# Retention outputs emitted in two steps with the state part last, and one weight block cast in four slices

## The chip, the cores and the metric

The kernel runs on one core of one Trainium2 chip. The metric is the device time of one execution on that core, in microseconds. "Span" is the time from the first to the last instruction in the profile; it is about 1.7 us shorter than the device time.

## The reference, cut to what matters

```python
# q, k, v: (8 batches, 8 heads, 576, 64), w_in: (512, 2048), w_out: (2048, 512)
scores = scale * np.matmul(q, k.transpose(0, 1, 3, 2))
ret = scores * Dmat[None]              # causal decay, gamma[h] ** (i - j) for i >= j
attn = np.matmul(ret, v)               # retention
x = attn.transpose(0, 2, 1, 3).reshape(8 * 576, 512)
r = np.maximum(x @ w_in, 0.0)
out = (r * r) @ w_out                  # feed-forward with squared ReLU
```

Retention over 576 positions is computed in chunks of 128: a masked product inside the chunk, plus a product of q with a state R that carries what came before the chunk. 4608 rows of x then go through the two dense layers, which are most of the work.

## The kernel before: the parts that matter

The program is a list of tasks for a scheduler that decides, before the program is built, in which order each engine gets them. A task has an engine, a key (the smallest key of the ready tasks goes first), an estimated duration, the tasks that it depends on, and buffers that it acquires. On the chip each engine then works in exactly that order, and waits on semaphores where the estimates were too short. So an edit of one task's key or duration can move instructions of other tasks.

Eight weight blocks of 1 MB are loaded as fp32 and cast to fp16, half by GpSimd (POOL in the profile), half by ScalarE (ACT):

```python
def add_weight(i):                      # blocks 0-3: w_in, 4-7: w_out
    ...
    halves = []
    for j, eng in enumerate(("POOL", "ACT")):
        rows, sl = (slice(0, 4), slice(256 * j, 256 * j + 256)) if i == 0 else (slice(2 * j, 2 * j + 2), slice(0, 512))

        def fc(eng=eng, rows=rows, sl=sl):
            s = tile_of["w", i]
            (nc.gpsimd.tensor_copy if eng == "POOL" else nc.scalar.copy)(out=dst[:, rows, sl], in_=s[:, rows, sl])
        key = -50 + i if i or j == 0 else -17.5
        halves.append(add(eng, key, 1.05 if eng == "POOL" else 1.0, fc, deps=[t]))
    sched.free("wst", halves)           # the staging buffer goes back
    wcast[i] = halves
```

For the first four groups of rows ("pairs") the retention outputs psO are one task of TensorE. The calls of inter need the state R; the loop of 32 small matmuls in the middle needs only the masked scores rx and the values vx:

```python
def fo():
    tile_of["psO", g] = ps_ret.tile([P, 2, 512], FP32, name="psO", tag="prO")
    inter(1)                            # with the state R
    nc.tensor.drain()
    for m in range(NP):                 # rx times vx: no state
        ...
    inter(0)                            # with the state before
t = add("PE", base + 24, 1.3, fo, deps=masked + [T["R", u]] + ([T["R", u - 1]] if carry else []), acq=("prO",))
```

The second dense layer of a group runs as two chains of 16 matmuls po, one for each half s of its rows. Matmul fi reads weight block 4 + fi // 4:

```python
for s, u in enumerate(us):
    ...
    for fi in range(NF):
        ...
        f2.append(add("PE", base2 + NF * s + fi, 0.216, f, deps=[sq[fi // nf]] + wcast[4 + fi // 4] + f2[-1:],
                      acq=("ff",) if fi == 0 else ()))
```

Last, wT is a set of weight differences that later groups use (they compute the layer with fewer products, Strassen's way). VectorE (DVE) works them out once all four w_out blocks are cast, and some of them sooner, between other work.

## Time and profile before

Before: 292.55 us median of 3 runs (292.39 to 292.78). The profile's own lines stand in the prediction. What they say about the start of the kernel fits into one table: when each weight block is ready in fp16 (end of POOL's half of the cast, start plus duration; ScalarE's half ends no later), and when TensorE starts the first matmul that reads it.

| block | POOL's cast ends, us | first matmul that reads it, us | slack |
|---|---|---|---|
| w_in 1 | 20.63 + 1.04 = 21.67 | 23.09 | 1.42 |
| w_in 2 | 23.55 + 1.04 = 24.59 | about 24.83 (16 matmuls of 0.109 after 23.09) | 0.24 |
| w_in 3 | 26.25 + 1.04 = 27.29 | 27.35 | a wait |
| w_out 0 | 28.95 + 1.04 = 29.99 | 30.41 | 0.42 |
| w_out 1 | 31.65 + 1.15 = 32.80 | 33.02 | 0.22 |
| w_out 2 | 34.32 + 1.04 = 35.36 | 35.63 | 0.27 |
| w_out 3 | 37.10 + 1.29 = 38.39 | 38.45 | a wait |

It is to be read as a row of gates. TensorE passes each gate no sooner than the block has landed and been cast.

### The profile page before, as it was taken

What the parts mean: (1) busy time and instruction counts of PE and PEld (TensorE: products, weight loads), DVE (VectorE), ACT (ScalarE), POOL (GpSimd) and SP (SyncE); (2) the same over time, 40 slices, a digit from 0 to 9 for tenths busy, and PEclk for the clock granted to TensorE, in tenths of its full rate; (3) what the DMA queues carried; (4) which work ended last, traced back from release to release, by engine and by line L of the source; (5) the groups of instructions that cost most, each with busy time, mean ns of one, the idle gap of its engine ahead of it and who ended that gap; (6) DMA issues with size and microseconds to landing.
All of it is one profiled execution on the core that took longest, in us unless ns stands there. A gap on an engine that the chain in (4) does not pass through costs nothing.

```text
span 290.9 us, 10062 instructions
## 1 busy us (share of the span) xinstructions
PE 283.0 (97%) x4328; PEld 234.0 (80%) x4328; DVE 195.0 (67%) x430; ACT 187.5 (64%) x354; POOL 88.9 (31%) x123
## 2 busy tenths in 40 slices
PE   7989999999999999999999999999999999999994
PEld 2557765688888888888888888888888888888883
DVE  3796589748485848656868857667786865565632
ACT  6456966296757575867666666766767676747830
POOL 5343454524434234251616041615151400000000
PEclk9999999999999999999999999999999999999999
DMA  7999999999999899997998599979896820201004
GB/s 201 327 368 387 370 276 250 239 220 186 233 214 214 185 148 247 221 186 189 196 208 180 126 192 211 202 183 180 211 188 171 159 74 2 74 3 72 2 2 144
DMA packets 139421, 54.13 MB, mean 186 GB/s; under 512 B 118129, under 2 KB 130929, under 8 KB 139377
## 3 DMA queue, kind: packets, MB, share of 16 engines
q1 hardware_dynamic: 139072, 53.23, 81.9%
q8 instruction: 34, 0.56, 0.9%
q10 hardware_dynamic: 304, 0.26, 0.3%
q14 instruction: 11, 0.08, 0.1%
HBM read 36.70 MB, written 9.44 MB: 159 GB/s over the span
## 4 chain that ended last, share of the span: by engine, by line
PE 89%; DMA 6%; SPq 1%; issue 1%; POOL 1%; DVE 0%; DVEq 0%; POOLq 0%
PE ph L827 42%; PE po L916 34%; PE po L865 5%; PE psO L343 4%; DMA wi<-in_moe_w_in_dram 3%; DMA pair<-in_q_dram 3%; PE psc L343 2%; PE psS L343 2%; SPq L298 1%; POOL w_in L322 1%; PE psT L418 1%; DVE o L939 0%; POOL qx L403 0%; DVE p L968 0%; DVEq L939 0%
## 5 line engine op out<-in xcount | busy, mean ns | idle before, releaser
L827 PE MATMUL ph<-xT,w_in 128*128 128x256 f16 x1152 | 139.4, 273 | 0.2 <-POOL w_in L322 0.2
L827 PEld LDWEIGHTS <-w_in 128*128 128x128 f16 x1152 | 111.1, 98 | 14.8 <-POOL w_in L322 0.4
L835 ACT ACTIVATE rl<-ph 128x512 f16<-128x512 f32 x144 | 84.3, 589 | 46.9 <-PE ph L827 45.0
L845 ACT ACTIVATE gT<-rl 128x512 f16<-128x512 f16 x104 | 65.6, 631 | 3.0
L916 PEld LDWEIGHTS <-gS 128*128 128x128 f16 x512 | 49.4, 98 | 6.1 <-DVE gS L893 0.2
L916 PE MATMUL po<-wT,gS 128*128 128x256 f16 x384 | 52.4, 273 | 0.0
L893 DVE TENSOR_TENSOR gS<-gT,gS 128x512 f16<-128x512 f16 x64 | 35.1, 554 | 11.6 <-ACT gT L845 11.0
L916 PEld LDWEIGHTS <-gT 128*128 128x128 f16 x384 | 37.2, 98 | 4.4
L893 DVE TENSOR_TENSOR gS<-gT 128x512 f16<-128x512 f16 x64 | 30.7, 481 | 12.9 <-ACT gT L845 12.9
L916 PE MATMUL po<-w_out,gT 128*128 128x256 f16 x256 | 34.5, 273 | 0.0
L355 POOL CAST kq<-q 128x512 f16<-128x512 f32 x28 | 18.8, 673 | 45.7 <-DMA q<-in_q_dram 45.5
L367 POOL TENSOR_TENSOR v<-v,vdec_full 128x512 f16<-128x512 f32 x24 | 26.2, 1093 | 19.6 <-DMA v<-in_v_dram 14.4
L355 POOL CAST kq<-k 128x512 f16<-128x512 f32 x28 | 18.6, 666 | 44.4 <-DMA k<-in_k_dram 41.7
L847 DVE TENSOR_TENSOR gT<-rl 128x512 f16<-128x512 f16 x40 | 18.9, 473 | 14.7 <-ACT rl L835 14.2
L929 ACT COPY u<-po 128x256 f32<-128x256 f32 x32 | 11.8, 369 | 20.4 <-PE po L916 20.4
L939 DVE TENSOR_TENSOR o<-po,u 128x256 f32<-128x256 f32 x31 | 13.0, 421 | 16.2 <-PE po L916 8.3
L704 DVE TENSOR_TENSOR xT<-psO,gam_full 128x512 f16<-128x512 f32 x28 | 18.9, 686 | 7.5 <-PE psO L343 7.4
L643 DVE TENSOR_TENSOR rT<-psc,mask 128x512 f16<-128x512 f32 x28 | 18.3, 683 | 5.5 <-PE psc L343 5.2
L916 PE MATMUL po<-w_out,gS 128*128 128x256 f16 x128 | 17.0, 273 | 0.0
L916 PE MATMUL po<-wT,gT 128*128 128x256 f16 x128 | 16.8, 273 | 0.0
L939 DVE TENSOR_TENSOR o<-po,p 128x256 f32<-128x256 f32 x17 | 7.2, 424 | 13.7 <-ACT u L929 7.1
L865 PE MATMUL po<-w_out,gT 128*128 128x512 f16 x64 | 15.8, 380 | 0.0
(81 smaller groups left out, 244.1 us busy)
## 6 DMA issues: line engine op xcount, KB each, us to landing
out_dram<-o SPq DMA_DIRECT2D x31, 256.0 KB, 3.0
k<-in_k_dram SPq DMA_DIRECT2D x24, 256.0 KB, 4.5
q<-in_q_dram SPq DMA_DIRECT2D x24, 256.0 KB, 4.8
v<-in_v_dram SPq DMA_DIRECT2D x24, 256.0 KB, 5.3
wi<-in_moe_w_in_dram SPq DMA_DIRECT2D x4, 1024.0 KB, 10.1
wo<-in_moe_w_out_dram SPq DMA_DIRECT2D x4, 1024.0 KB, 9.7
pair<-in_k_dram SPq DMA_DIRECT2D x4, 512.0 KB, 7.0
pair<-in_q_dram SPq DMA_DIRECT2D x4, 512.0 KB, 7.0
```

The lines of the kernel that those rows point to most:

```text
L343: nc.tensor.matmul(out_, lhsT=lhsT, rhs=rhs, start=start, stop=True, skip_group_check=True, tile_position=(64 * row, 64 * col))
L355: op(out=out_.rearrange("p (n b a d) -> p n b a d", n=2, b=2, a=2), in_=in_.rearrange("p (n a b) d -> p n b a d", n=2, a=2))
L367: nc.gpsimd.tensor_tensor(out=t, in0=tile_of["v32", u], in1=vdec[kind].rearrange("p (h o) -> p h o", o=1).to_broadcast([P, H, D]), op=ALU. ...
L704: nc.vector.tensor_tensor(out=tile_of["x", g][:, :, s * P:(s + 1) * P].rearrange("p n (c i) -> p c n i", c=2), in0=tile_of["psO", g][:, :, ...
L827: nc.tensor.matmul(tile_of["ph", g, fb][:, j, :], lhsT=w_in16[:, m, fi * P:(fi + 1) * P], rhs=tile_of["x", g][:, m, :], start=(m == 0), st ...
L835: nc.scalar.activation(out=t, in_=tile_of["ph", g, fb], func=ACTF.Relu)
L845: nc.scalar.activation(out=t, in_=rl, func=ACTF.Square)
L847: nc.vector.tensor_tensor(out=t, in0=rl, in1=rl, op=ALU.mult)
L865: nc.tensor.matmul(tile_of["po", u], lhsT=tile_of["g", g][:, fi, s * P:(s + 1) * P], rhs=w_out16[:, fi, :], start=(fi == 0), stop=(fi == N ...
L893: nc.vector.tensor_tensor(out=Sx(k, h), in0=in0(h), in1=in1(h), op=op)
L916: nc.tensor.matmul(tile_of["pb", g, bank], lhsT=left(i), rhs=right[:, i, :], start=(start and i == 0), stop=(i == HF - 1), skip_group_chec ...
L939: nc.vector.tensor_tensor(out=o_tile(u)[:, half * HM:(half + 1) * HM], in0=bank(x), in1=tile_of[name, g], op=ALU.add)
```

## The change

Its intent: the 32 products that need no state are to run while VectorE still works on R, so that less TensorE work is left behind R, and the dense matmuls start sooner. So that the second weight block is no obstacle then, its cast is cut into four slices, and the first matmuls wait only for the slice that they read. The key of the first pair's R is raised too. Left out are the keys of the casts (ScalarE's raised by 0.1, and so on slice by slice) and the estimated durations of the slices, divided by 1.85. The core of the diff:

```diff
+    NARROW = (1,)
...
-        for j, eng in enumerate(("POOL", "ACT")):
-            rows, sl = (slice(0, 4), slice(256 * j, 256 * j + 256)) if i == 0 else (slice(2 * j, 2 * j + 2), slice(0, 512))
+        narrow = i in NARROW
+        for j, eng in enumerate(("POOL", "ACT", "POOL", "ACT") if narrow else ("POOL", "ACT")):
+            rows, sl = ((slice(0, 4), slice(128 * j, 128 * j + 128)) if narrow else
+                        (slice(0, 4), slice(256 * j, 256 * j + 256)) if i == 0 else (slice(2 * j, 2 * j + 2), slice(0, 512)))
...
-            chain.append(add("DVE", base + 5.6 + s, 0.5, fr2, deps=[t] + chain[-1:], acq=("R",)))
+            chain.append(add("DVE", base + (6.5 if u == 0 else 5.6) + s, 0.5, fr2, deps=[t] + chain[-1:], acq=("R",)))
...
-        def fo():
+        def fo1():
+
             tile_of["psO", g] = ps_ret.tile([P, 2, 512], FP32, name="psO", tag="prO")
-            inter(1)
-            nc.tensor.drain()
             for m in range(NP):
...
+        def fo2():
             inter(0)
-        t = add("PE", base + 24, 1.3, fo, deps=masked + [T["R", u]] + ([T["R", u - 1]] if carry else []), acq=("prO",))
+            nc.tensor.drain()
+            inter(1)
+        t = add("PE", base + 23.9, 0.6, fo1, deps=masked + T["kvx", u], acq=("prO",))
+        t = add("PE", base + 24, 0.75, fo2, deps=[t, T["R", u]] + ([T["R", u - 1]] if carry else []))
...
-        return w[:1] if fi < 2 else w
+        return w[fi % 4:fi % 4 + 1] if fi // 4 in NARROW else w[:1] if fi < 2 else w
```

More of the change, by code (lines that the diff above doesn't have):

```diff
@@ L322, in fc @@
                 (nc.gpsimd.tensor_copy if eng == "POOL" else nc.scalar.copy)(out=dst[:, rows, sl], in_=s[:, rows, sl])
-            key = -50 + i if i or j == 0 else -17.5
-            halves.append(add(eng, key, 1.05 if eng == "POOL" else 1.0, fc, deps=[t]))
+            key = -50 + i + 0.1 * j if i or j == 0 else -17.5
+            halves.append(add(eng, key, (1.05 if eng == "POOL" else 1.0) / (1.85 if narrow else 1), fc, deps=[t]))
         sched.free("wst", halves)
```

## The prediction

> **What bounds the kernel now.** I read the page first, then who waited for whom on TensorE, then the timelines of TensorE and of the engines that feed it from 14 to 40 us, because an order listing of the two programs shows no instruction moved after about 57 us.
>
> ```profile
> span 290.9 us, 10062 instructions
> PE 283.0 (97%) x4328; PEld 234.0 (80%) x4328; DVE 195.0 (67%) x430; ACT 187.5 (64%) x354; POOL 88.9 (31%) x123
> PE   7989999999999999999999999999999999999994
> ...
> GB/s 201 327 368 387 370 276 250 239 220 186 233 214 214 185 148 247 221 186 189 196 208 180 126 192 211 202 183 180 211 188 171 159 74 2 74 3 72 2 2 144
> ```
>
> TensorE is busy for 97% of the span, so no other engine's total matters; what can be won is the part in which it is not yet fed. One slice is 7.3 us: only the first four hold less than full work, and they also hold 40 warming matmuls that give nothing. In the second to fifth slice the transfers run at 327 to 387 GB/s, by far their highest: inputs and eight weight blocks of 1 MB come in as fast as this program ever moves data.
>
> ```profile
> PE psO L343 <- DVE R L489: 0.9, 1, 0.9
> PE ph L827 <- POOL w_in L322: 0.2, 1, 0.2
> ```
>
> These two are the waits of TensorE that the change can touch: one for the state R ahead of the outputs of the second pair, one for a weight cast. Now the same in order of time:
>
> ```profile
> 20.02 1.04 PE L247 MATMUL warm<-junk 128*128 128x512 f16 x4
> 22.00 0.31 PE L343 MATMUL psO<-kqT,R 64*64 64x128 f16 x8 [0.94 <-DVE R L489]
> 22.41 0.64 PE L343 MATMUL psO<-rx,vx 64*64 64x128 f16 x32
> 22.87 0.29 PE L343 MATMUL psO<-kqT,R 64*64 64x128 f16 x8
> 23.09 4.10 PE L827 MATMUL ph<-xT,w_in 128*128 128x256 f16 x36
> 27.35 3.23 PE L827 MATMUL ph<-xT,w_in 128*128 128x256 f16 x28 [0.15 <-POOL w_in L322]
> ...
> 36.50 1.91 PE L827 MATMUL ph<-xT,w_in 128*128 128x256 f16 x16
> 38.45 3.18 PE L865 MATMUL po<-w_out,gT 128*128 128x512 f16 x14
> ```
>
> From 23.09 on TensorE has real work with one gap of 0.15 us. The columns are start, duration, engine, line, what it writes from what, count, and in brackets the idle time before. The outputs psO hold TensorE from 22.00 to 23.09, and the 32 products in the middle of them do not need R. What feeds it:
>
> ```profile
> 20.93 1.02 DVE L489 TENSOR_TENSOR R<-stmp,dec 128x256 f16<-128x256 f32 x1
> 20.63 1.04 POOL L322 CAST w_in<-wi 128x1024 f16<-128x1024 f32 x1 [1.56 <-DMA wi<-in_moe_w_in_dram]
> 23.55 1.04 POOL L322 CAST w_in<-wi 128x1024 f16<-128x1024 f32 x1 [1.88 <-DMA wi<-in_moe_w_in_dram]
> 28.95 1.04 POOL L322 CAST w_out<-wo 128x1024 f16<-128x1024 f32 x1 [1.66 <-DMA wo<-in_moe_w_out_dram]
> 36.80 0.69 DVE L778 TENSOR_TENSOR wT<-w_out 128x1024 f16<-128x1024 f16 x1
> 37.10 1.29 POOL L322 CAST w_out<-wo 128x1024 f16<-128x1024 f32 x1 [1.74 <-DMA wo<-in_moe_w_out_dram]
> ```
>
> Every weight cast of POOL ends a wait for its transfer. The last one ends at 37.10 + 1.29 = 38.39, and the first matmul that reads its block starts at 38.45. That coincidence carries my prediction: the ph before it end at 38.41, so in the kernel before TensorE arrives at this block just as it is ready.
>
> **What the Trainium skill says.** First, "SBUF — State Buffer", section "Who interferes with whom": VectorE's tensor_tensor with both inputs in SBUF and a GpSimd instruction that reads SBUF exclude each other for a whole instruction, and one with at most one SBUF input does not contend outside the 2-port modes. The trace agrees: R<-stmp,dec took 1.02 us beside POOL's cast and 0.42 at 22.51 without one; POOL's last cast took 1.29 instead of 1.04, with wT running at its start. Second, "TensorE: Matmul & The Clock Gate", section "Step-by-step: what each phase is for": only weight loads are pulled ahead; "The MATMULs themselves stay in program order". So a matmul that waits for a block holds back all work queued behind it; the trace shows it at 22.00, where 0.94 us pass while w_in matmuls stand behind. Third, "DMA: Bandwidth & Descriptors", section "Queues, rings and completion order": each of the 16 engines takes descriptors in ring order, though completion is not first in, first out. The landings here fit that: POOL's casts of successive blocks start 2.7 to 2.9 us apart from 20.63 to 37.10.
>
> **The change, part by part.** It removes no work: the same count of matmuls, casts differ only in cut.
>
> (a) First pair. Products go first and R last, and the outputs now stand ahead of the second pair's transposes of q. The four masks on VectorE run in a row from 10.37 (4 x 0.64), so products start near 13.0, R is ready near 13.4 and psO ends near 14.2 against 14.92; xT gains 0.7 us. But the transposes of q slide from 13.25 to about 14.2, ScalarE's copies of them end near 15.9 instead of 14.96, and its half of the first weight cast, which stood at 15.03, ends near 16.9 instead of 16.07. The matmuls at 17.27 come perhaps 0.4 us earlier, and then TensorE waits for vx in any case, which ended at 18.10 + 1.53 = 19.63 because v landed at 18.0. That gain falls into warming matmuls: 0 us on the path.
>
> (b) Second pair. The 32 products move into the time before R, when TensorE ran warming matmuls or stood idle. VectorE's order changes: two masks after vx instead of one, and the square gT moves behind the R chain. So R starts at 19.55 + 2 x 0.64 + 0.41 = 21.24 instead of 20.93, but the old one only lost its time to the lock; the new one meets POOL's second slice, and ends between 21.65 and 22.0. Left behind it are 16 small matmuls and the drain, about 0.6 us by the rows at 22.00 and 22.87, instead of 1.09. The w_in matmuls start near 22.2 to 22.6 instead of 23.09: 0.5 to 0.9 us earlier.
>
> (c) Slices. The second block's cast takes the same 1.04 us in two halves per engine, ready slice by slice from about 21.2 instead of 21.67. As the path in (b) arrives at 22.2 or later, the whole block is there already: 0 us.
>
> (d) What follows, with 1.74 us for 16 ph (33.02 - 31.28) and 0.87 for 4 po, both from starts in the timeline of before. From the later start, 22.6: block 1 takes until 24.35. Block 2's cast ends at 23.55 + 1.04 = 24.59: TensorE waits 0.25 us (0.65 from the early start). From 24.62 come 28 ph, which the new order puts ahead of block 3: 3.05, to 27.67; block 3 is ready at 27.29. Then 20 ph: 2.18, to 29.85. First w_out block: 28.95 + 1.04 = 29.99, a wait of nearly 0.2. From 30.03: 4 po and 20 ph to 33.08, 4 po and 16 ph to 35.69, 4 po and 12 ph to 37.87. The last w_out block is ready at 38.39, if its cast is: TensorE waits nearly 0.6 us and starts at 38.45, as before.
>
> (e) Does the last block come earlier? It lands at 37.1, after a backlog of blocks issued long before; nothing in the change frees a staging buffer earlier, and the first weight cast frees its one 0.8 us later. Its cast is held to 38.39 by wT, which comes after the square of a block whose ReLU follows ScalarE's cast of the third w_out block at 34.29, again a landing. So this too stays. Sum: 0.5 to 0.9 us won at 23 us, all of it returned by 38.45; 0 us net, with 0.25 us to be had if wT and the cast do not collide.
>
> **The rivals.** One: the 0.5 us comes through to the end, 292.0 us. For it speaks that the kernel is otherwise bound by TensorE and that the pairs' outputs stand directly ahead of the dense work. Against it stands the row at 37.10. Two: the last cast escapes the lock and ends at 38.14; then 0.25 us comes through, 292.3. The narrow margin, 36.80 against 37.10, makes this possible. Three: a loss. ScalarE's later cast delays the third w_in block's place in the ring, or the moved transposes make a later copy late; each 0.1 us of later landing at 37.1 costs 0.1 us, since everything behind is bound by TensorE. The backlog speaks against it; I give it up to 0.4 us, 292.9. The later two pairs use the new order too, but there products, R and drain stand in a full queue with the same sum of matmuls: I count nothing.
>
> **Range and chances.** Centre: 292.55 less about 0.1, for a share of rival two: 292.45 us. Three runs of before spread over 0.39 us, and the rivals span 292.0 to 292.9, so 291.95 to 292.95 should hold it. A change of 2% is 5.85 us; nothing that the change touches is that long: same 0.98, faster 0.01, slower 0.01.
>
> **What would show it.** Right: w_in matmuls of the second block start about 0.5 us earlier than 23.09; new waits of TensorE for POOL's casts of w_in and w_out, about 1 us together, the longest ahead of the last w_out block; po x14 at 38.45 within 0.15. Step (b) is wrong if psO still ends near 23; (d) if the 14 po start without a wait; (e) if POOL's last cast starts or ends more than 0.2 us from 37.10 and 38.39. If the span falls by 0.5 us or more, the last block was not the gate.

## The result

| | before | after |
|---|---|---|
| median, us | 292.66 (292.39 to 292.97, 4 runs) | 292.85 (292.58 to 293.44, 4 runs) |
| ratio after / before | | 1.0009, 95% interval 0.999 to 1.0027 |
| span of the profiled run, us | 290.9 | 291.1 |

A ratio here is always the mean time of one kernel's fast runs over the mean of the other's in the same rounds, so it is not quite the ratio of the medians beside it. Five more rounds of the same changed kernel on another set gave 292.65 against 292.6, ratio 1.0004 (0.999 to 1.0018). The change makes no difference of 2%, and none that these runs resolve at all.

First, TensorE's timeline of the kernel after. The columns are as in the prediction: start, duration, engine, line, what it writes from what, count, idle time before.

```profile
21.15 0.64 PE L347 MATMUL psO<-rx,vx 64*64 64x128 f16 x32
21.73 0.39 PE L247 MATMUL warm<-junk 128*128 128x512 f16 x1
22.05 0.71 PE L347 MATMUL psO<-kqT,R 64*64 64x128 f16 x16
22.69 7.46 PE L835 MATMUL ph<-xT,w_in 128*128 128x256 f16 x64
30.11 1.02 PE L873 MATMUL po<-w_out,gT 128*128 128x512 f16 x4
...
36.63 1.47 PE L835 MATMUL ph<-xT,w_in 128*128 128x256 f16 x12
38.41 3.18 PE L873 MATMUL po<-w_out,gT 128*128 128x512 f16 x14 [0.30 <-POOL w_out L326]
41.42 0.61 PE L422 MATMUL psT<-ident,kx 128*128 128x128 f16 x8
```

The products run at 21.15, ahead of R; the part with R follows at 22.05; the w_in matmuls start at 22.69 instead of 23.09. That is the intended gain: 0.40 us. But the last two rows stand almost exactly where the kernel before had them: the 14 po at 38.41 instead of 38.45, and the transposes behind them at 41.42 instead of 41.46. The gain of 23 us is gone by 38 us. In its place stands a wait of 0.30 us that the kernel before did not show, for the last w_out block. What feeds TensorE, POOL and VectorE of the kernel after:

```profile
20.97 1.36 POOL L326 CAST w_in<-wi 128x512 f16<-128x512 f32 x2 [1.15 <-DMA wi<-in_moe_w_in_dram]
37.14 1.21 POOL L326 CAST w_out<-wo 128x1024 f16<-128x1024 f32 x1 [1.71 <-DMA wo<-in_moe_w_out_dram]
```

```profile
20.98 0.88 DVE L493 TENSOR_TENSOR R<-stmp,dec 128x256 f16<-128x256 f32 x1
36.77 0.69 DVE L786 TENSOR_TENSOR wT<-w_out 128x1024 f16<-128x1024 f16 x1
```

The last cast ends at 37.14 + 1.21 = 38.35 (before: 38.39), and the matmuls that wait for it start 0.06 us later. The list of what TensorE waited for, in microseconds in total, times, and the longest:

```profile
PE ph L835 <- POOL w_in L326: 0.8, 1, 0.8
...
PE po L873 <- POOL w_out L326: 0.3, 1, 0.3
```

The wait of 0.94 us for R is gone from it. The 0.8 us stand at 17.74, where the first w_in block landed late in this execution, and it takes the place of warming matmuls; in the second profile of the same kernel it was not there. The chain that ended last, in this stretch (start, duration, what):

```profile
23.64 1.05 POOL w_in L326
...
24.71 9.62 DMA wo<-in_moe_w_out_dram
...
34.39 1.04 POOL w_out L326
35.43 1.68 issue
...
37.14 1.22 POOL w_out L326
...
38.41 3.18 PE po L873 x14
```

The path to the end runs through transfers and casts until 38.41, not through the matmuls before it. POOL's cast at 23.64 frees a staging buffer, a transfer starts that lasts until 34.34, and so on: none of these links was touched by the change. (The 1.68 us of "issue" ahead of the last cast are, by POOL's own row above, its wait for the transfer of the last block.)

### The profile page after: what moved, and what is told of

It is laid out like the page before. It is cut to its first block, busy times and chain, and to the rows that moved or that the text cites. A ratio compares the mean times of both kernels' runs of the same rounds, so it can differ in the third digit from the quotient of the medians.

```text
span 291.1 us, 10066 instructions
## 1 busy us (share of the span) xinstructions
PE 283.5 (97%) x4328; PEld 234.2 (80%) x4328; DVE 197.1 (68%) x430; ACT 187.2 (64%) x355; POOL 91.7 (32%) x124
## 4 chain that ended last, share of the span: by engine, by line
PE 85%; DMA 9%; POOL 1%; SPq 1%; issue 1%; DVE 0%; DVEq 0%; POOLq 0%
PE ph L835 39%; PE po L924 34%; PE po L873 4%; PE psO L347 4%; DMA wi<-in_moe_w_in_dram 4%; DMA wo<-in_moe_w_out_dram 3%; DMA pair<-in_q_dram 2%; PE psc L347 2%; PE psS L347 2%; SPq L298 1%; POOL w_out L326 1%; PE psT L422 1%; POOL w_in L326 0%; DVE o L947 0%; POOL qx L407 0%
## 5 line engine op out<-in xcount | busy, mean ns | idle before, releaser
L901 DVE TENSOR_TENSOR gS<-gT,gS 128x512 f16<-128x512 f16 x64 | 36.9, 583 | 12.1 <-ACT gT L853 11.5
L359 POOL CAST kq<-q 128x512 f16<-128x512 f32 x28 | 19.6, 700 | 47.9 <-DMA q<-in_q_dram 47.7
L359 POOL CAST kq<-k 128x512 f16<-128x512 f32 x28 | 20.0, 715 | 40.2 <-DMA k<-in_k_dram 38.2
L855 DVE TENSOR_TENSOR gT<-rl 128x512 f16<-128x512 f16 x40 | 20.6, 515 | 14.4 <-ACT rl L843 13.7
```

What stands on the lines that cost most here:

```text
L359: op(out=out_.rearrange("p (n b a d) -> p n b a d", n=2, b=2, a=2), in_=in_.rearrange("p (n a b) d -> p n b a d", n=2, a=2))
L855: nc.vector.tensor_tensor(out=t, in0=rl, in1=rl, op=ALU.mult)
L901: nc.vector.tensor_tensor(out=Sx(k, h), in0=in0(h), in1=in1(h), op=op)
```

## The experiments

Theory: the outputs in two steps do start the dense work earlier, and the last w_out block takes the gain back, because its landing and its cast do not depend on TensorE. Rivals: the gain would come through to the end; or the slices or the moved work cost something that cancels it.

The kernels of the runs told together ran on one chip and share their runs of the kernel before: first set (median of before 292.6) after_again, e3, e4, e5; second set (292.7) e7, e8, e9, e1; third set (292.77) e4_again, e6, e2.

### after_again: the changed kernel once more, unchanged

> The changed kernel once more, so that it stands on the same chip as the next three runs. Theory (the landing of the last w_out block and its cast are the gate): within 0.3 us of before, w_in matmuls of the second block start near 22.7, then the 14 po matmuls start near 38.4 after a wait of 0.3 to 0.5 us for POOL's cast. Rival A (the change costs something of its own, as its 0.2 us longer median suggests): 0.2 to 0.5 us slower than before again.

Measured: 292.65 us, ratio 1.0004 (0.999 to 1.0018). The 14 po started at 38.49 with a wait of 0.33 us, so the gate is there again. The w_in matmuls started at 22.54. The first landing was the early one this time, POOL's first cast at 15.05 instead of 16.64, and the 0.8 us wait at 17.74 was gone. The extra 0.2 us of the first medians was not reproduced.

### e1_outputs_only and e2_slices_only: each part of the change alone

e1 is the kernel after without the slices; e2 is the kernel before with nothing but the slices.

```diff
-    NARROW = (1,)
+    NARROW = ()
```

> The outputs in two steps without the slices. Theory: the slices lie beside the path, so this does what the whole change does: w_in matmuls of the second block near 22.7 and a span within 0.2 us of the changed kernel. Rival E (the slices feed the earlier start): these matmuls start later than 22.9.

> The slices without the outputs in two steps. Theory: TensorE still waits for R ahead of all of psO, so w_in matmuls of the second block start where they do in before (22.4 to 23.1, by which of R and POOL's cast takes the lock first), and the total is that of before within 0.2 us. Rival E (the slices are the useful part): start near 22 and a shorter time.

Measured: e1 292.74 us, ratio 0.9999 (0.9985 to 1.0012), with the w_in matmuls at 22.35 and the 14 po at 38.23 behind a wait of 0.31 us: the walk of the kernel after, without the slices. e2 292.72 us, ratio 0.9999 (0.9985 to 1.0013). Neither part does anything to the time.

e2 taught more than it was built for. It has the old order of the outputs, and yet its timelines of TensorE, VectorE and POOL show:

```profile
21.03 0.31 PE L347 MATMUL psO<-kqT,R 64*64 64x128 f16 x8
...
22.12 1.92 PE L831 MATMUL ph<-xT,w_in 128*128 128x256 f16 x16
24.44 2.36 PE L831 MATMUL ph<-xT,w_in 128*128 128x256 f16 x20 [0.40 <-POOL w_in L326]
```

```profile
20.55 0.42 DVE L493 TENSOR_TENSOR R<-stmp,dec 128x256 f16<-128x256 f32 x1
```

```profile
20.60 1.40 POOL L326 CAST w_in<-wi 128x512 f16<-128x512 f32 x2 [1.05 <-DMA wi<-in_moe_w_in_dram]
```

There is no wait for R, and the w_in matmuls start at 22.12, earlier than in any profile of the new order. R took 0.42 us because it started 0.05 us ahead of POOL's cast; in the profile of before, the cast had started at 20.63, 0.30 us ahead of R, and R took 1.02. This is a race between VectorE and GpSimd for their shared port, and all thirteen profiles show it: R took 0.42 or 0.43 us in the eight in which it started before POOL's cast (by 0.01 to 0.14 us) and 0.87 to 1.31 us in the five in which it started after (by 0.01 to 0.55 us). The wait for R that the change set out to remove stands in two of the four profiles with the old order (0.94 us in before, 0.91 in e5) and not in the other two (e2 and e9): it belongs to executions, not to the kernel. With the gain already there, e2 waits twice for w_in casts, 0.40 us at 24.44 and 0.34 us at 27.14, and its 14 po start at 38.23, right after its last cast (36.90 + 1.28 = 38.18).

### e3_late_wT: keep the wT difference away from the last cast

```diff
-            ts.append(add("DVE", 3 * L + i, 0.85, f, deps=sum((wcast[j] for j in range(4, 8)), [])))
+            ts.append(add("DVE", 3 * L + i, 0.85, f, deps=sum((wcast[j] for j in range(4, 8)), []), lag=1.0))
```

> The changed kernel with VectorE's first wT subtraction moved behind the last cast of w_out. Theory: POOL's last cast is no longer held by the lock and takes 1.04 us instead of 1.21, so it ends at 38.18 and the 14 po matmuls start near 38.2 instead of 38.4: 0.15 to 0.2 us shorter than the changed kernel. Rival B (the lock plays no part, ScalarE's half of the cast is the gate): POOL's cast 1.2 us still, no change of start.

Measured: 292.73 us (292.62 to 292.94), ratio 1.0004 (0.9991 to 1.0016). POOL's timeline, then TensorE's:

```profile
37.23 1.04 POOL L326 CAST w_out<-wo 128x1024 f16<-128x1024 f32 x1 [1.71 <-DMA wo<-in_moe_w_out_dram]
```

```profile
38.33 3.18 PE L873 MATMUL po<-w_out,gT 128*128 128x512 f16 x14
```

Without wT beside it the last cast takes 1.04 us, and the po follow its end at once: 38.33, against 38.49 in after_again, whose block landed at nearly the same time (cast start 37.21). So the lock on the last cast is shown, and it costs 0.16 us at this place. In the time nothing of it is to be seen; five rounds resolve some 0.4 us (the interval spans 0.0025 of 292.6, 0.7 us), not 0.16.

### e7_late_block: let the last block land later

Two extra loads of 256 KB each are put into the transfer queue just ahead of the last w_out block:

```diff
+        if i == 7:
+            def fz():
+                for n in range(2):
+                    z = o_pool.tile([P, DM], FP32, name="extra", tag="o")
+                    nc.sync.dma_start(out=z, in_=w_out[n * P:(n + 1) * P, :])
+            dma_task(0, 1.38, fz)
```

> The changed kernel with 0.5 MB of useless loads queued just ahead of the last w_out block. Theory: the block lands 1.35 us later (0.52 MB at 387 GB/s), the 14 po matmuls start near 39.8 and the kernel takes 1.2 to 1.5 us more. Rival (TensorE is bound by its own work from 23 us on, transfers are hidden): less than 0.3 us more.

Measured: 293.96 us (293.79 to 294.38), ratio 1.0037 (1.0022 to 1.0052), so 1.08 us more. TensorE's timeline:

```profile
39.99 3.18 PE L879 MATMUL po<-w_out,gT 128*128 128x512 f16 x14 [2.04 <-POOL w_out L332]
```

The cast of the block ended at 38.61 + 1.33 = 39.94, and TensorE had waited 2.04 us for it. Against the kernel before, whose po started at 38.45, they are 1.54 us later. In this execution all of it reached the end: the last row of po<-wT,gS starts at 286.79, against 285.19 in before. So the last block is a gate whose delay counts. The extra loads also push back the transfers queued behind the block, but the transposes of the next rows follow the po after 3.02 us (43.01), as in the kernel after (3.01), so nothing else held TensorE there. The profiled execution was the slowest of the four (294.38); the median's 1.08 us, a little under the expected 1.2 to 1.5, comes from executions that were not profiled.

### e8_half_last_block and e9_before_half_last_block: open the gate

Only half of the last block is loaded, and the cast reads that half twice over, so that it lands earlier while every instruction behind it stays. e8 does it to the kernel after, e9 to the kernel before. **The results are wrong on purpose** (relative error 0.499).

```diff
-                nc.sync.dma_start(out=t, in_=w_out[fb * 512:(fb + 1) * 512, :].rearrange("(n p) m -> p n m", p=P))
+                m = 2 if i == 7 else 4
+                nc.sync.dma_start(out=t[:, 0:m], in_=w_out[fb * 512:fb * 512 + m * P, :].rearrange("(n p) m -> p n m", p=P))
```

> The changed kernel, but only the first half of the last w_out block is loaded and used twice, so the result is wrong on purpose. Theory: the block lands 1.35 us earlier, TensorE waits no longer for it: 0.3 to 0.5 us less than the changed kernel. Rival C (a later gate collects the time): no change.

> The same half load in the kernel before, wrong result on purpose. Theory: no wait there, so within 0.15 us of before; with the run above, the change is then worth 0.3 to 0.5 us once the gate is away. Rival: it gains as much as the run above, so the change itself is worth nothing even without the gate.

Measured: e8 292.45 us, ratio 0.9994 (0.998 to 1.0007); e9 292.36 us, ratio 0.9991 (0.9978 to 1.0005). TensorE's timeline of e8, with a row from further on, then VectorE's row ahead of that:

```profile
37.76 3.19 PE L874 MATMUL po<-w_out,gT 128*128 128x512 f16 x14
...
67.75 0.61 PE L925 MATMUL po<-wT,gS 128*128 128x256 f16 x4 [0.40 <-DVE gS L902]
```

```profile
66.51 1.19 DVE L902 TENSOR_TENSOR gS<-gT,gS 128x512 f16<-128x512 f16 x1
```

The last cast now starts at 35.73, and the 14 po start at 37.76 without a wait, 0.65 us earlier than in the kernel after. In e9 they start at 38.24. So with the gate open, the two orders are 0.48 us apart at this place in these two executions. It is not R that parts them: in e9, too, R won the race, and the w_in matmuls started at 22.40, in e8 at 22.33. But e9 waited at two w_in blocks, 0.32 us at 24.64 and 0.34 us at 27.35, and from there on it stood where before had stood. e8 waited only once, 0.30 us at 24.55: the new order of outputs has led the scheduler to put more ph ahead of block w_in 3 (28 from the gate of w_in 2 on, where the old order has 20), so that block is ready when TensorE comes to it.

The times do not follow. e9 was to stay within 0.15 us of before and came out about 0.3 lower; e8 was to be clearly faster than e9 and is not. Both intervals hold 1, so the rival for e9, that the change is worth nothing even without the gate, is not excluded by the times.

The profile of e8 (293.03 us, near the slowest of its five) shows one place where its lead went. At 67.75 TensorE waits 0.40 us for VectorE's gS. That addition took 1.19 us, and the like one at 67.95 takes 0.41; it had started 0.14 us after POOL's multiplication of v (66.37, 1.04 us). By these rows it is the same race once more and not only the price of coming early, though no run tested it: e4's TensorE came to this place at 67.03, earlier still, found its gS done (0.43 us from 65.89) and did not wait. In e8 the lead over before fell from 0.68 us at the transposes (40.78 against 41.46) to 0.10 behind this wait (68.64 against 68.74); by the last row of po<-wT,gS it was 0.37 us behind (285.56 against 285.19), and for that part the profile lists no wait. e9 (profiled at 293.1, its slowest) lists a wait of 0.17 us for gS too, but at 214.12. The profiles of before and of after list none.

### e4_reorder, e4_again and e5_before_reorder: work to bridge the gate

Nothing is left out here. Two po of the second half of the rows, which read the long-ready first w_out block, are moved ahead of the four po that need the last block, so that TensorE has 0.43 us of work at the gate. e4 is the kernel after with this order in group 0, e4_again is the same file again, e5 is the kernel before with it.

```diff
-        for s, u in enumerate(us):
-            end = base2 + NF * (s + 1)
-            f2 = T["ff2"][-1:] if s == 0 else f2[-1:]
-            for fi in range(NF):
+        f2 = T["ff2"][-1:]
+        done = {}
+        for s, lo, hi in ((0, 0, 12), (1, 0, 2), (0, 12, NF), (1, 2, NF)) if g == 0 else ((0, 0, NF), (1, 0, NF)):
+            u = us[s]
+            late = g == 0 and s == 1 and lo == 0
+            for fi in range(lo, hi):
...
-                f2.append(add("PE", base2 + NF * s + fi, 0.216, f, deps=[sq[fi // nf]] + wcast[4 + fi // 4] + f2[-1:],
-                              acq=("ff",) if fi == 0 else ()))
+                f2.append(add("PE", 95 if late else base2 + NF * s + fi, 0.216, f,
+                              deps=[sq[fi // nf]] + wcast[4 + fi // 4] + f2[-1:], acq=("ff",) if fi == 0 else ()))
+            done[s] = f2[-1]
```

> The changed kernel with two po matmuls of the second token block, whose weights have long arrived, moved ahead of the four po matmuls that wait for the last w_out block. Theory: they fill 0.43 us of the wait, so everything behind comes about 0.4 us earlier and the kernel takes 0.4 us less than the changed one, near 292.3. Rival C (the wait is not lost time because a later gate, the casts of the next k, collects it): TensorE waits ahead of the transposes of kx instead, total unchanged.

> The kernel before with the same two po matmuls moved. Theory: the kernel before reaches the last w_out block just as it is ready and has no wait there to fill, so 0 us (within 0.15). Rival D (any filler ahead of that block helps, whatever the change did): the same 0.4 us as in the changed kernel.

> The changed kernel with the two po matmuls moved, once more on another chip. Theory: 292.2 to 292.6 us again, 0.1 to 0.4 us under before of the same rounds and no wait for POOL's cast ahead of the last w_out block. Rival (the first result was chance): within 0.1 us of the changed kernel's 292.7 to 292.9.

Measured: e4 292.5 us, ratio 0.9993 (0.998 to 1.0006); e4_again 292.54 us, ratio 0.9992 (0.9978 to 1.0006); e5 292.77 us, ratio 1.0005 (0.9993 to 1.0018). TensorE's timeline of e4:

```profile
37.77 3.68 PE L875 MATMUL po<-w_out,gT 128*128 128x512 f16 x16
```

The block of 16 starts at 37.77 where the kernel after waited until 38.41. Two fillers of 0.22 us take it to 38.2, and the last cast ended at 37.01 + 1.21 = 38.22: the wait is filled. The transposes behind come at 41.29 with two more po done than in the kernel after, whose transposes came at 41.42. Together that is 0.13 + 0.43, about 0.56 us of progress, and in these two executions the last rows of po<-wT,gS are as far apart (284.77 against 285.33). Against before, 0.60 us at the transposes were 0.42 at that row. The medians of e4 show 0.1 to 0.2 us of it, and its interval holds 1 in both sets. With the same filler the kernel before gains nothing in its time. In its profile, R lost the race and the ph ahead of the gate started 0.33 us later than in before (36.83 against 36.50), but at the transposes it was only 0.14 us behind (41.17 with two po fewer done, against 41.46). So the filler covered some 0.2 us of a wait that the expectation had denied; step (d) below comes to the same wait. The direction is the theory's (with the gate bridged, the new order is the faster one), but neither run alone settles it.

### e6_narrow12_reorder: e4 with two blocks in slices

```diff
-    NARROW = (1,)
+    NARROW = (1, 2)
```

> The same, and the third w_in block cast slice by slice too, because TensorE waits 0.25 to 0.4 us for that cast in every trace of the changed kernel. Theory of gates in a row: that wait shrinks to less than 0.15 us and 28 ph come earlier, but the first four po still start when the first w_out block is cast, near 29.9, so the total equals the run above within 0.15 us. Rival (each wait taken away is time won): 0.25 us less than the run above.

Measured: 292.46 us (291.99 to 292.49), ratio 0.9985 (0.9972 to 0.9997). This is the best of all correct kernels here and the only one whose interval lies wholly below 1: about 0.4 us, 0.15%. It is one of twelve comparisons, so chance is not excluded. The slices of block 2 removed the wait at 24.5 us that e4 had, as meant. But the weight loads of block 3 then waited 0.37 us for its cast, and the first po came at 29.92 against 29.94 in e4: each gate passed early only leads to the next. Its profiled execution also waited 0.28 us for gS at 67.45, an addition that took 0.80 us. So the profile does not explain why e6 measured 0.2 us below e4 in the mean, and that difference is left open.

## Why the prediction was right or wrong

The time was predicted as 292.45 us and came out as 292.85 in its own rounds and 292.65 in the repeat, inside the range 291.95 to 292.95; "same" was right. Step by step:

**(a) First pair, nothing on the path: right.** With the early landing (after_again, e1) the first w_in matmuls, and with them everything up to the wait for vx, fell into the time of warming matmuls. ScalarE's half of the first cast came later, as worked out: 15.77 in after_again instead of 15.03; 16.9 had been estimated for its end, 15.77 + 1.06 = 16.83 was measured.

**(b) Second pair, 0.5 to 0.9 us at 23 us: right in direction for the profiled pair, too large, and measured against a start that is not fixed.** The w_in matmuls started at 22.69, just outside the predicted 22.2 to 22.6, and the gain was 0.40 us. The step took the old 23.09 as given. But with the old order and R winning the race, e2 started at 22.12 and e9 at 22.40, and with R losing (1.31 us) e5 started at 23.65. The new order started between 22.33 and 22.82 in nine profiles, whether R took 0.42 or 0.89 us. That R lost in the one profile that the step was built on was one outcome of the race: with the old order it lost in two profiles of four (see e2). So at this place the change narrows the spread, from 1.5 us to 0.5, and gains nothing on an execution in which R wins. A reason can be read from the rows, though no run tested it: in after_again R ended at 20.83 + 0.42 = 21.25, but the part with R started only at 21.90, behind the products (21.00 to 21.58) and a warming matmul.

**(c) The slices, 0 us: right.** e1 and e2 both measured 0.9999.

**(d) The walk through the gates: right in its sum, off in one term.** The predicted waits ahead of the first po, 0.25 and nearly 0.2 us, are there: from 22.69, 64 ph of 0.109 us would last until 29.67, and the po came at 30.11, 0.44 us later. (The profile books none of it as TensorE's idle time in this execution; in after_again it shows 0.34 us.) The wait at the last block appeared in after, after_again and e1, and the 14 po, predicted at 38.45, came at 38.41. What was mis-sized is the term that carried the argument in "What bounds the kernel now": that the ph ahead of the last block end at 38.41 and that "in the kernel before TensorE arrives at this block just as it is ready". The end of a matmul row is modelled. Starts tell more. Two rows of the kernel before:

```profile
33.89 1.91 PE L827 MATMUL ph<-xT,w_in 128*128 128x256 f16 x16
35.63 1.03 PE L865 MATMUL po<-w_out,gT 128*128 128x512 f16 x4
```

Sixteen ph take 35.63 - 33.89 = 1.74 us from start to start, although the row says 1.91. From 36.50 the next po could thus have started at 38.24, and they started at 38.45: the kernel before already waited 0.21 us at the last block, and the profile showed none of it, because the modelled end covered it. e9 is the test: there the gate is open, the ph start at 36.50 too, and the po follow at 38.24.

```profile
38.24 3.18 PE L866 MATMUL po<-w_out,gT 128*128 128x512 f16 x14
```

In the kernel after, twelve ph of 0.109 us lead from 36.63 to 37.94, and the po started at 38.41, a wait of 0.47 of which the profile shows 0.30. Now the gain can be followed in full. Of 0.40 us at 22.69, 0.10 went at the gates ahead of the first po (0.44 us of waits, against 30.41 - 23.09 - 6.98 = 0.34 before), 0.26 went at the last block (0.47 against 0.21), and 0.04 was left, 38.41 against 38.45.

The Trainium skill could have prevented this: "Perfetto Trace Analysis", section "Tensor Engine Instruction (MATMUL, LD_WEIGHTS)", says that TensorE's end times are estimated from the instruction's size and not observed. The trace fits: the row of 16 ph ends 0.17 us after the time at which the next matmul could start (1.91 against 1.74).

**(e) The last block does not come earlier: right.** Its cast started at 37.10 before and at 37.14 and 37.21 after. e7 shows that this gate reaches the end of the kernel, and e3 shows that wT stretches the cast.

**The rivals.** One, the gain comes through: not with the gate in place. With the gate bridged (e4) or open (e8) the medians fell by 0.1 to 0.25 us, less than TensorE's lead at 38 to 41 us. In the profiles, e4 keeps most of its lead to the end; e8 loses 0.58 us of it at 67 us, by its rows to the port race, and more than the rest later. Two, the cast escapes the lock: its 0.1 us in the centre was not earned; in the profiles of the kernel after the last cast took 1.21 and 1.23 us. Three, a loss: the first 1.0009 looked like it, the repeat and e1 do not bear it out.

What stays open: why the medians of e4 and e8 show less than the lead of their profiles at 41 us; where the profiled e8 lost the other 0.47 us behind 68 us; whether the change is worth anything once the gate is away; and anything smaller than 0.1%, which these rounds do not resolve.

## What to carry to other kernels

Before counting on an earlier start, list the gates behind it, here the casts of weight blocks that transfers alone decide, and find the last one without slack: a gain is worth what it is worth there. Measure TensorE's waits from start to start, not from the modelled ends, or a gate of 0.2 us passes for none. And when a change is aimed at a wait of under a microsecond in one profile, look at a second execution first: this wait was the lost half of a race.

## What the Trainium skill lacked or had wrong

- "SBUF — State Buffer", section "Who interferes with whom", says that the order of issue decides who blocks. The runs agree, and add how little decides: R started 0.01 us ahead of the cast in e4 and took 0.42 us while POOL's two slices took 1.44; in the kernel after it came 0.01 us behind and took 0.88. The section does not say how a trace shows the loss: as a longer instruction, not as idle time before it (the last cast 1.29 us beside wT, 1.04 without it in e3).
- "Perfetto Trace Analysis", section "Tensor Engine Instruction (MATMUL, LD_WEIGHTS)", calls the end an estimate but does not say that it can hide a wait: here a row of 16 ph is booked as 1.91 us where 1.74 pass from start to start, and of a wait of 0.21 us only 0.04 is left between the booked end and the next start.
- No page that was read gives the time from the end of a GpSimd cast to the start of the matmul that waits for it: here 0.05 to 0.06 us, in every kernel in which the last block was the gate.
- No page that was read speaks of a landing that differs this much between executions of the same order of transfers: POOL's first weight cast started at 14.9 to 15.1 us in ten of the thirteen profiles and at 16.6 to 16.9 in three, before and after the change alike. What decides it was not found.
